# A ring of stationary operands set 192 bytes into its tiles, and eight sums of squares with 64 moving columns

## The chip, the core and the metric

The kernel runs on one core of a Trainium2 chip, in one launch. The metric is the device time of the whole program in microseconds; the median of three runs before the change is 837.2 us (836.03 to 839.48). TensorE (PE in the profile) multiplies: a weight load (PEld) puts a stationary operand of 128x128 into the array, and a matmul then streams the moving operand's columns past it into PSUM. VectorE is DVE, ScalarE is ACT, GpSimd is POOL, and SP issues most DMAs.

## The reference

Linear attention without a softmax, RMS normalisation per head, and a feed-forward block with GELU, all in fp32:

```python
kv  = np.einsum('bhsd,bhse->bhde', k, v)          # 8 batches, 8 heads, 576 tokens, 64 wide
out = np.einsum('bhsd,bhde->bhse', q, kv)
rms = np.sqrt(np.mean(out * out, axis=-1, keepdims=True) + 1e-06)
x   = (out / rms * g_norm)                        # taken as 4608 tokens x 512
h   = x @ w_in                                    # 512 -> 2048
g   = 0.5 * h * (1.0 + erf(h / sqrt(2)))
return g @ w_out                                  # 2048 -> 512
```

## The kernel before

The 4608 tokens go through in nine chunks of 512 (`CH`), eight heads as four pairs. Products of fp32 accuracy are made of three fp32r matmuls with split operands: high with high, low with high, high with low. A fp32r matmul is one pass of the array; one of plain fp32 stands in the profile as two.

The prologue treats the first chunk. Ten plain products of the zero tile `warm` (`keep_warm`, L638) keep TensorE going until the first loads land. A product of one row of ones with one row of `eps` (L691) lays D times epsilon over the first 48 columns of a PSUM tile `sums`. The kv sums (`sum_kv`, L151), the projections (`project_first`, L672) and their squares on ScalarE follow. For pairs 2 and 3 `sum_squares` (L683) adds the squares up with TensorE: a block of 128 tokens is the stationary operand, and `heads`, two columns of ones and noughts, is the moving operand; it writes two columns of `sums` for each of eight blocks. `rsqrt` works on the 48 columns, and products with `ident` (L739) spread the result.

The first two chunks (`PLAIN`) run with weight tiles that are split on the way: `layer1` (L529) and `layer2` (L555), both with 512 moving columns. Meanwhile sums of weight blocks are written to DRAM tiles called `products`.

The other seven chunks (from chunk 2 on) take the first layer by `layer1_pair`: for each of eight pairs j of blocks it does seven products of half size, each of six fp32r matmuls of 256 moving columns (L436). That is 42 matmuls a pair, 56 pairs, 2352 matmuls. The stationary operand of such a product comes from a ring of four tiles, `w_in0` to `w_in3`, filled in turn from `products` by `load_products` (L419); the moving operand is a split piece of x, which lies in the tiles x0 to x5 or w_in5 to w_in12. Behind a pair come the projections of the next chunk (`project`, L211) in some places, then 24 matmuls of layer 2 with 512 columns. The order is written out by hand; every engine works in the order of its own code, SP's loads too.

All tiles lie behind one another in SBUF in the order in which their names first occur, each at a start address of its own, the same in every partition. A tile of the ring has 4096 bytes a partition, as has every weight tile. The starts in the built program, in bytes of a partition, and the rest when divided by 256:

| tiles | role | start before | rest |
|---|---|---|---|
| w_in0, w_in1, w_in2, w_in3 (ring) | stationary in L436 | 59072, 63168, 71360, 91840 | 192 |
| x0 to x5 | moving in L436 and L529 | 157376 to 177856, steps of 4096 | 192 |
| w_in5 to w_in9; w_in10 to w_in12 | moving in L436 in even; in odd chunks | 108224 to 140992, steps of 8192; 26304, 79552, 153280 | 192 |
| kv_h0, kv_h1, kv_l0, kv_l1 | stationary in L211 | 16512, 18560, 20608, 22656 | 128 |
| qh, ql, w_in4 | moving in L211 | 198592, 200640, 100032 | 192 |
| gh, gl | stationary in L555 | 202688 and on | 192 |
| w_out0 to w_out15 | moving in L555 | 67264 and others | 192 |

Within these tiles the operands of L436 and L555 begin at multiples of 512 bytes, those of L211 at multiples of 256 bytes. So in L436, L529 and L555 a stationary and a moving operand have the same rest; in L211 the rests are 128 and 192.

Of the kernel before, what the change touches and what calls it, by code (L numbers as in the profile page):

```python
# [8 lines left out]
F32 = mybir.dt.float32  # L9
F32R = mybir.dt.float32r  # L10
I32 = mybir.dt.int32
AF = mybir.ActivationFunctionType
# [4 lines left out]
P = 128  # L17
EPS = 1e-6
CH = 512
KROWS = 112  # L20
WARM = 10
PLAIN = 2
HALF = CH // 2
RING = 4
# [11 lines left out]
def linear_attn_rms_gelu_ffn(  # L36
# [16 lines left out]
    nc = tc.nc  # L53
    ctx.enter_context(tc.manual_schedule())
    NT, DM = out.shape
# [5 lines left out]
    NF = w_in.shape[0]  # L61
# [4 lines left out]
    const = ctx.enter_context(tc.tile_pool(name="const", bufs=1))  # L66
# [6 lines left out]
    HI, LO = slice(0, DM), slice(DM, 2 * DM)  # L73
    kv_h = [const.tile([P, NP, P], F32R, name=f"kv_h{s}") for s in range(2)]
    kv_l = [const.tile([P, NP, P], F32R, name=f"kv_l{s}") for s in range(2)]
    ident = const.tile([P, P], F32, name="ident")
    fold = const.tile([P, P], F32, name="fold")
    warm = const.tile([P, P], F32, name="warm")
    half_g = const.tile([P, 1], F32, name="half_g")
    heads = const.tile([P, 2], F32, name="heads")  # L80


    kv_in, late = {}, {}
# [1 line left out]
    def late_tile(name):  # L85

        if name not in late:
            late[name] = const.tile([P, 2 * DM], I32, name=name).bitcast(F32)
        return late[name]
# [18 lines left out]
    def load_kv(b, p):  # L108

        early = b == 0 or (b == 1 and p > 1)  # L110
        if early:
            main = late_tile(f"w_out{NF - 1 - p if b == 0 else NF - 3 - p}")
        elif b == PLAIN + 1 and p > 1:
            main = const.tile([P, 2 * DM], F32, name=f"w_in{8 + p}")
# [9 lines left out]
        else:  # L124
            if early:
                tail = late_tile(f"w_in{NF - 5}")[:, (p - 2) * 2 * P:(p - 1) * 2 * P]
            elif b == PLAIN + 1 and p > 1:
                if p == 2:
# [38 lines left out]
    class Attn:  # L167
# [22 lines left out]
        def split_q(self, p, eng=nc.gpsimd):  # L190
            q = self.q.pop(p)
            if self.c > PLAIN and p % 2:
                t = const.tile([P, 2 * DM], F32R, name="w_in4")
# [150 lines left out]
    kept = {}  # L344

    def reused(i, dtype=F32):

        if i not in kept:
            kept[i] = const.tile([P, 2 * DM], dtype, name=f"w_in{i}")
        return kept[i]  # L350

    def piece_tile(c, n):
        k = (["x2", "x3"] + [f"w_in{i}" for i in range(5, 10)],
# [40 lines left out]
    def high_sums():  # L394

        for (j, second), s in stage.items():
            if j % 2:
                t = reused(second, F32R).rearrange("p (k a n) -> p k a n", k=2, a=2)
            else:
                t = const.tile([P, 2, 2, HALF], F32R, name=f"x{2 + second}")  # L400
            nc.scalar.copy(out=t[:, :, 0], in_=s)
            halved[j, second] = s, t
        stage.clear()
# [10 lines left out]
    ring = {}  # L414

    def load_products(t):
        if t < (NCH - PLAIN) * NT2:
            ring[t] = reused(t % RING, F32R)
            nc.sync.dma_start(out=ring[t].bitcast(F32), in_=products[t % NT2])  # L419

    def layer1_pair(at, j, between):
# [8 lines left out]
        def product(k, out, first=False):  # L430
            n = ((at.c - PLAIN) * NF // 2 + j) * NPR + k
            w, x = ring[n // 2][:, n % 2 * DM:(n % 2 + 1) * DM], at.x[k]
            for kb in range(2):
                hi, lo = (w[:, m * HALF + kb * P:m * HALF + (kb + 1) * P] for m in range(2))
                for i, (y, z) in enumerate(((hi, 0), (lo, 0), (hi, 1))):
                    nc.tensor.matmul(  # L436
                        out=out, lhsT=y, rhs=x[:, z, kb], start=first and kb + i == 0,
                        stop=kb == 1 and i == 2, skip_group_check=True,
                    )
            if n % 2:  # L440
                load_products(n // 2 + RING)
# [25 lines left out]
    raw, parts = {}, {}  # L467

    def load_w(n):
        kind, i = weights[n]  # L470
        src = w_in[i] if kind == "in" else w_out[i * P:(i + 1) * P, :]
        raw[n] = const.tile([P, 2 * DM], I32, name=f"w_{kind}{i}")
        nc.sync.dma_start(out=raw[n], in_=src.bitcast(I32))

    zs, ws = {}, {}
# [27 lines left out]

    def high_w(n):
        kind, i = weights[n]
        t = const.tile([P, 2 * DM], F32R, name=f"w_{kind}{i}")
        parts[kind, i] = t
        nc.scalar.copy(out=t[:, HI], in_=ws[n].bitcast(F32))

# [89 lines left out]

    attn = [Attn(c) for c in range(NCH)]  # L600
    first, second = attn[:2]
    nc.vector.memset(warm, 0.0)
    nc.scalar.activation(out=heads, in_=warm[:, :2], func=AF.Gelu)
    mask, g_row = late_tile(f"w_in{NF - 6}")[:, :P], late_tile(f"w_in{NF - 6}")[:1, P:2 * P]
    nc.gpsimd.memset(mask, 0.0)
    ones, eps = (late_tile(f"w_in{NF - 6}")[:1, a * P:(a + 1) * P] for a in (2, 3))
# [10 lines left out]
    for h in range(2):  # L617
        nc.scalar.dma_start(out=g_row[:, h * D:(h + 1) * D], in_=g_norm.unsqueeze(0))
    load_w(0)
    for p in range(2):  # L620
        load_kv(1, p)
    for n in (1, 2, 3):
        load_w(n)
    for p in (2, 3):
        load_kv(1, p)
    load_w(4)
    second.load(0)
    for n in range(5, 9):
# [7 lines left out]
    def keep_warm(count):  # L636
        for _ in range(count):
            nc.tensor.matmul(out=dummy[:, :P], lhsT=warm, rhs=warm, start=True, stop=True)  # L638

    sums = ps_h.tile([P, CH], F32, name="ps_h")  # L640
    dummy = ps_h.tile([P, CH], F32, name="ps_h")
    keep_warm(WARM)
    nc.gpsimd.memset(heads, 0.0)
# [5 lines left out]
    for d in range(0, 2 * D, BLK):  # L649
        h = d // D * D  # L650
        nc.gpsimd.tensor_tensor(
            out=fold[:, d:d + BLK], in0=ident[:, h:h + BLK], in1=ident[:, h + BLK:h + 2 * BLK],
# [7 lines left out]
    sq, NG = {}, CH // P  # L660
# [17 lines left out]
    n = 2 * NB  # L678


    def sum_squares(p):
        for k in range((p - 2) * NG, (p - 1) * NG):
            nc.tensor.matmul(  # L683
                out=sums[:, n + 2 * k:n + 2 * k + 2],
                lhsT=sq[p][:, k % NG * P:(k % NG + 1) * P], rhs=heads, start=False, stop=True,
                skip_group_check=True,
            )

    first.part = work.tile([P, NP, NB], F32, name="part")

    nc.tensor.matmul(  # L691
        out=sums[:, :n + 4 * NG], lhsT=ones, rhs=eps[:, :n + 4 * NG], start=True, stop=False,
        skip_group_check=True,
    )
    sum_first(0)
# [3 lines left out]
        out=half_g, in0=ps[:, :1], scalar1=0.5, scalar2=None, op0=ALU.mult  # L699
# [3 lines left out]
        out=root_g, in0=half_g, scalar1=D ** 0.5, scalar2=None, op0=ALU.mult  # L703
# [8 lines left out]
    for p in (2, 3):  # L712
        project_first(p)
    top_w(0)
    bits_w(0)
    sum_squares(2)
    nc.tensor.matmul(
        out=sums[:, :n].rearrange("p (g b) -> p g b", g=2), lhsT=fold, rhs=first.part[:, :2, :],
        start=False, stop=True, skip_group_check=True,
    )  # L720
    sum_squares(3)
    for p in (2, 3):
        nc.scalar.activation(
            out=first.o_tile(p), in_=first.ps.pop(p), func=AF.Copy, scale=root_g
# [9 lines left out]
    for p in (2, 3):  # L734
        bcs[p] = ps_acc.tile([P, DM], F32, name=f"acc{p}")
        for t in range(NG):
            for h, r in enumerate((slice(0, D), slice(D, 2 * D))):
                k = n + 2 * ((p - 2) * NG + t) + h
                nc.tensor.matmul(  # L739
                    out=bcs[p][r, t * P:(t + 1) * P],  # L740
                    lhsT=first.inv[:, k:k + 1].broadcast_to((P, D)), rhs=ident,
                    start=True, stop=True,
                )
    for p in range(2):
# [3 lines left out]
            out=first.o_tile(p), in0=first.ps.pop(p), scalar=root_g, in1=bc, op0=ALU.mult,  # L748
# [16 lines left out]
    g, h, acc, sums = {}, {}, {}, {}  # L765
# [90 lines left out]
    def convert(i, gelu_rest, between):  # L856

        count = 3 if i in (2, 4, 6, 8) else 2 if i < 11 else i in (11, 12, 14)  # L860
        now = [order.pop(0) for _ in range(count)]
        for k, n in enumerate(now or [None]):
            if last:
                high_w(last[0])
                if last[0] + 2 < len(weights):
                    top_w(last[0] + 2)
            if not i and not k:
                gelu_rest()
                low_w(last.pop())
            if n is not None:  # L870
                bits_w(n)
            if i and not k:
                gelu_rest()
            if last:
                low_w(last.pop())
            if n is not None:
                last.append(n)
            if not k:
                between()
# [6 lines left out]

    for s in range(PLAIN * NF):
        c, i = divmod(s, NF)
# [7 lines left out]
        if c == 0:  # L896
# [4 lines left out]
            def between():  # L901
                if i == 0:
                    for p in (2, 3):
                        attn[0].low_x(p, nc.vector)
                if i in (9, 10):
                    high_w(i - 9)
                    low_w(i - 9)
                if i == 1:
                    split_kv(1, range(NP))
                    nc.scalar.copy(out=kv_h[0], in_=kv_f)  # L910
                    nc.vector.tensor_tensor(
                        out=kv_l[0], in0=kv_f, in1=kv_h[0].bitcast(F32), op=ALU.subtract
                    )
                spread_work(c, i)
# [9 lines left out]
        else:  # L924
# [3 lines left out]
            n = 0 if not 1 <= i <= 11 else 2 if i in (1, 3, 5, 7, 11) else 1  # L928
# [114 lines left out]
```

## Time and profile before

The profiled execution took 835.6 us, of which the span that the profile covers is 833.8 us; 1.8 us lie around it.

| what | value |
|---|---|
| runs | 836.03, 837.2, 839.48 us |
| profiled execution | 835.6 us, span 833.8 us, mean granted clock 0.999 |
| TensorE matmuls | 5386, 828.9 us busy |
| DVE, ACT, POOL busy | 495.9, 314.2, 65.5 us |
| DMA | 174.97 MB, mean 210 GB/s |

A matmul's own duration in the profile includes its way through the array, so the durations of consecutive matmuls overlap. What a matmul costs in a stream is the time from its start to the start of the next. The timeline gives starts in us; a row that merges x24 matmuls gives the start of the first.

### The profile page before, as it was taken

Reading aid. Unit: us, or ns where it says so; the run is one execution under the profiler, and the core shown is the slowest. Engines: PE = TensorE matmul, PEld = TensorE weight load, DVE = VectorE, ACT = ScalarE, POOL = GpSimd, SP = SyncE. Lnnn points to the kernel's source line nnn. Section 1 sums busy time; section 2 is a strip of 40 time slices with the busy share of each in tenths; the row PEclk is TensorE's granted clock in tenths of the full one; section 3 lists DMA queues with packets and bytes.
Section 4 is the critical chain, followed back from the end, with each engine's and each line's share of the span. In section 5 each row is a group of like instructions: output and inputs, shape, how many; then the busy total and the mean of one; then the engine's idle time right before and its main releaser. Section 6 shows DMA issues by size and latency. Waiting matters only on the chain.

```text
span 833.8 us, 13801 instructions
## 1 busy us (share of the span) xinstructions
PE 828.9 (99%) x5386; PEld 735.0 (88%) x5386; DVE 495.9 (59%) x980; ACT 314.2 (38%) x578; POOL 65.5 (8%) x69
## 2 busy tenths in 40 slices
PE   9999999999999999999999999999999999999998
PEld 7688888888999999999999999999999989999997
DVE  3999838687546744674457545673467446744443
ACT  3788444434532334233423253233323332322221
POOL 1000021011000101010001010010101000100000
PEclk9999999999999999999999999999999999999999
DMA  9981347776784568455945587456555655556551
GB/s 348 407 330 51 114 135 250 254 245 240 252 304 135 180 230 307 161 177 202 339 159 176 199 281 262 151 177 229 172 172 172 232 188 177 177 177 227 177 177 51
DMA packets 61605, 174.97 MB, mean 210 GB/s; under 512 B 6500, under 2 KB 15460, under 8 KB 61540
## 3 DMA queue, kind: packets, MB, share of 16 engines
q1 hardware_dynamic: 61536, 174.09, 60.0%
q8 instruction: 43, 0.70, 0.3%
q14 instruction: 22, 0.18, 0.1%
q10 hardware_dynamic: 4, 0.00, 0.0%
HBM read 149.95 MB, written 24.12 MB: 209 GB/s over the span
## 4 chain that ended last, share of the span: by engine, by line
PE 99%; DVE 0%; issue 0%; ACT 0%; DVEq 0%
PE acc L555 47%; PE ps_h L436 34%; PE ps_h L529 10%; PE ps_a L211 3%; PE ps_a L151 2%; PE ps_h L521 1%; PE ps_h L638 1%; PE acc L672 0%; PE acc L739 0%; PE ps_h L683 0%; PE ps_a L241 0%; DVE w L594 0%; DVE w_in L664 0%; PE ps_h L691 0%; DVE sq L583 0%
## 5 line engine op out<-in xcount | busy, mean ns | idle before, releaser
L555 PE MATMUL acc<-w_out,gh 128*128 128x512 f32 x700 | 217.0, 391 | 0.0
L436 PE MATMUL ps_h<-w_in,w_in 128*128 128x256 f32 x1392 | 176.2, 283 | 0.0
L436 PEld LDWEIGHTS ps_h<-w_in,w_in 128*128 128x128 f32 x1392 | 171.1, 192 | 0.0
L555 PE MATMUL acc<-w_out,w_in 128*128 128x512 f32 x672 | 159.7, 392 | 0.0
L555 PEld LDWEIGHTS acc<-w_out,gh 128*128 128x128 f32 x700 | 129.3, 188 | 25.5
L555 PEld LDWEIGHTS acc<-w_out,w_in 128*128 128x128 f32 x672 | 124.0, 188 | 24.8
L555 PE MATMUL acc<-w_out,gl 128*128 128x512 f32 x350 | 136.3, 390 | 0.0
L541 ACT ACTIVATE gh<-ps_h 128x512 fp32r<-128x512 f32 x88 | 52.7, 599 | 212.6 <-DVE ps_h L428 155.4
L436 PEld LDWEIGHTS ps_h<-x,w_in 128*128 128x128 f32 x960 | 122.6, 191 | 4.4
L436 PE MATMUL ps_h<-x,w_in 128*128 128x256 f32 x960 | 123.9, 283 | 0.0
L541 ACT ACTIVATE w_in<-ps_h 128x512 fp32r<-128x512 f32 x56 | 33.6, 600 | 184.7 <-DVE ps_h L428 184.7
L446 DVE COPY w_in<-ps_h 128x256 f32<-128x256 f32 x56 | 23.8, 425 | 133.1 <-PE ps_h L436 133.1
L428 DVE TENSOR_TENSOR ps_h<-ps_h,w_in 128x256 f32<-128x256 f32 x168 | 72.7, 432 | 48.0 <-PE ps_h L436 43.6
L428 DVE TENSOR_TENSOR w_in<-ps_h,w_in 128x256 f32<-128x256 f32 x168 | 71.4, 425 | 49.2 <-PE ps_h L436 47.2
L529 PE MATMUL ps_h<-x,w_in 128*128 128x512 f32 x360 | 86.8, 390 | 0.0
L547 DVE TENSOR_TENSOR gl<-ps_h,gh 128x512 fp32r<-128x512 f32 x88 | 60.4, 687 | 42.4 <-ACT ps_h L542 38.0
L542 ACT ACTIVATE ps_h<-ps_h 128x512 f32<-128x512 f32 x144 | 85.5, 594 | 0.0
L529 PEld LDWEIGHTS ps_h<-x,w_in 128*128 128x128 f32 x360 | 67.4, 188 | 13.9 <-POOL x L299 0.2
L555 PEld LDWEIGHTS acc<-w_out,gl 128*128 128x128 f32 x350 | 65.7, 188 | 14.1
L547 DVE TENSOR_TENSOR w_in<-ps_h,w_in 128x512 fp32r<-128x512 f32 x56 | 38.4, 686 | 17.1 <-ACT ps_h L542 17.1
L199 POOL TENSOR_TENSOR ql<-q,qh 128x512 fp32r<-128x512 f32 x16 | 21.1, 1321 | 211.5 <-ACT qh L198 140.9
L334 POOL TENSOR_TENSOR w_in<-o,w_in 128x512 fp32r<-128x512 f32 x13 | 16.9, 1325 | 210.8 <-ACT w_in L329 210.8
(153 smaller groups left out, 640.4 us busy)
## 6 DMA issues: line engine op xcount, KB each, us to landing
w_in<-products SPq DMA_DIRECT2D x196, 512.0 KB, 4.6
products<-w_in SPq DMA_DIRECT2D x40, 256.0 KB, 3.0
w_in<-w_in SPq DMA_DIRECT2D x16, 512.0 KB, 10.2
kv_main<-kv_main SPq DMA_DIRECT2D x16, 512.0 KB, 7.0
w_out<-w_out SPq DMA_DIRECT2D x16, 512.0 KB, 10.2
q<-qT SPq DMA_DIRECT2D x15, 512.0 KB, 5.7
out<-w SPq DMA_DIRECT2D x18, 256.0 KB, 2.1
out<-z SPq DMA_DIRECT2D x17, 256.0 KB, 2.3
```

Source lines behind the costliest of these rows:

```text
L151: nc.tensor.matmul(out=ps[r, n * D:(n + 1) * D], lhsT=k[:, r], rhs=v[:, r], start=(j == 0), stop=(j == NJ),)
L199: eng.tensor_tensor(out=ql, in0=q, in1=qh.bitcast(F32), op=ALU.subtract)
L211: nc.tensor.matmul(out=ps[:, a:e], lhsT=w, rhs=x[:, a:e], start=(m == 0), stop=(m == 2))
L334: eng.tensor_tensor(out=x[:, 1], in0=self.block(OPERANDS[n]), in1=x[:, 0].bitcast(F32), op=ALU.subtract,)
L428: add = lambda out, x, y: nc.vector.tensor_tensor(out=out, in0=x, in1=y, op=ALU.add)
L436: nc.tensor.matmul(out=out, lhsT=y, rhs=x[:, z, kb], start=first and kb + i == 0, stop=kb == 1 and i == 2, skip_group_check=True,)
L446: nc.vector.tensor_copy(out=p1, in_=a[:, left])
L529: nc.tensor.matmul(out=h, lhsT=parts["in", i][:, w][:, p * P:(p + 1) * P], rhs=at.x[p][:, x], start=(m + p == 0), stop=(m == 2 and p == NP ...
L541: nc.scalar.activation(out=gh, in_=h, func=AF.Gelu)
L542: nc.scalar.activation(out=h, in_=h, func=AF.Gelu)
L547: nc.vector.tensor_tensor(out=gl, in0=h, in1=gh.bitcast(F32), op=ALU.subtract)
L555: nc.tensor.matmul(out=ps, lhsT=x[:, ts], rhs=parts["out", i][:, w], start=(i == 0 and m == 0), stop=(m == 2 and (i == NF - 1 or (i, t) == ...
```

## The change

Three things change in the code.

1. **The ring.** The four ring tiles get 64 more fp32 columns (256 bytes). `load_products` writes a product pair 48 columns (192 bytes) behind the tile's start, and the products read it there. What else uses these tiles still begins at their start.
2. **The sums of squares.** `heads` gets 72 columns, all nought but the first two. `sum_squares` streams the first 64 of them and so writes 64 columns of `sums`, the last 62 with an addend of nought. The product with `eps` covers 128 columns in place of 48, so that all of these columns are begun.
3. **Room.** `ident` and `warm` (512 bytes each) give up tiles of their own and lie in the tile w_in10, which is loaded with weights later.

```diff
+WIDE = 64
-    ident = const.tile([P, P], F32, name="ident")
-    warm = const.tile([P, P], F32, name="warm")
-    heads = const.tile([P, 2], F32, name="heads")
+    heads = const.tile([P, 72], F32, name="heads")
+    AWAY, ROOM = 48, 64
+    def block_tile(name, dtype):
+        ring = name in [f"w_in{i}" for i in range(RING)]
+        return const.tile([P, 2 * DM + (ROOM if ring else 0)], dtype, name=name)
...
     def load_products(t):
         if t < (NCH - PLAIN) * NT2:
-            ring[t] = reused(t % RING, F32R)
+            reused(t % RING, F32R)
+            ring[t] = kept[t % RING][:, AWAY:AWAY + 2 * DM]
             nc.sync.dma_start(out=ring[t].bitcast(F32), in_=products[t % NT2])
...
+    ident = late_tile(f"w_in{NF - 6}")[:, DM + 2 * P:DM + 3 * P]
+    warm = late_tile(f"w_in{NF - 6}")[:, DM + P:DM + 2 * P]
...
         for k in range((p - 2) * NG, (p - 1) * NG):
             nc.tensor.matmul(
-                out=sums[:, n + 2 * k:n + 2 * k + 2],
-                lhsT=sq[p][:, k % NG * P:(k % NG + 1) * P], rhs=heads, start=False, stop=True,
+                out=sums[:, n + 2 * k:n + 2 * k + WIDE],
+                lhsT=sq[p][:, k % NG * P:(k % NG + 1) * P], rhs=heads[:, :WIDE], start=False, stop=True,
                 skip_group_check=True,
             )
...
-        out=sums[:, :n + 4 * NG], lhsT=ones, rhs=eps[:, :n + 4 * NG], start=True, stop=False,
+        out=sums[:, :P], lhsT=ones, rhs=eps, start=True, stop=False,
```

In the built program the ring's tiles now start at 58304, 62656, 71104 and 91840, again with a rest of 192, so a product's stationary operand, 192 bytes further, has a rest of 128. Every other tile in the table keeps its rest. The pair of rests in L436 is now 128 and 192, as in L211.

No engine gets its instructions in another order. TensorE's rows around the sums of squares (`ql` and `gh` hold the squares of pairs 2 and 3, `part` the reduced squares of pairs 0 and 1) stood before as

```order
L672 MATMUL acc_315<-w_in_130,w_in_153 128x512
L683 MATMUL ps_h<-heads,ql 128x2 x4
L717 MATMUL ps_h<-part,fold 128x32
L683 MATMUL ps_h<-heads,gh 128x2 x4
L638 MATMUL ps_h<-warm 128x128 x2
```

and stand now as

```order
L682 MATMUL acc_313<-w_in_128,w_in_151 128x512
L694 MATMUL ps_h<-heads,ql 128x64 x4
L728 MATMUL ps_h<-part,fold 128x32
L694 MATMUL ps_h<-heads,gh 128x64 x4
L648 MATMUL ps_h<-w_in_109 128x128 x2
```

Only the shape of eight rows and the name of the zero tile differ. The first pair of chunk 2 reads the ring (the right one of the two operands) before as

```order
L436 MATMUL ps_h<-x_1971,w_in_1483 128x256 x6
L436 MATMUL ps_h<-x_2068,w_in_1483 128x256 x6
L436 MATMUL ps_h<-w_in_2071,w_in_1492 128x256 x6
L436 MATMUL ps_h<-w_in_2152,w_in_1492 128x256 x6
L436 MATMUL ps_h<-w_in_2017,w_in_2049 128x256 x6
L436 MATMUL ps_h<-w_in_2020,w_in_2049 128x256 x6
L436 MATMUL ps_h<-w_in_2155,w_in_2051 128x256 x6
```

and now, with the same count, shapes and order,

```order
L444 MATMUL ps_h<-x_1969,w_in_1481 128x256 x6
L444 MATMUL ps_h<-x_2066,w_in_1481 128x256 x6
L444 MATMUL ps_h<-w_in_2069,w_in_1490 128x256 x6
L444 MATMUL ps_h<-w_in_2150,w_in_1490 128x256 x6
L444 MATMUL ps_h<-w_in_2015,w_in_2047 128x256 x6
L444 MATMUL ps_h<-w_in_2018,w_in_2047 128x256 x6
L444 MATMUL ps_h<-w_in_2153,w_in_2049 128x256 x6
```

The load of w_in10 with weights waits for TensorE's last read of `ident` besides the engines that it waited for; the product that reads `g_norm`'s row (L697) waits for ScalarE besides its DMAs.

More of the change, by code (lines that the diff above doesn't have):

```diff
@@ L348, in reused @@
         if i not in kept:
-            kept[i] = const.tile([P, 2 * DM], dtype, name=f"w_in{i}")
-        return kept[i]
+            kept[i] = block_tile(f"w_in{i}", dtype)
+        return kept[i][:, :2 * DM]
     def piece_tile(c, n):
@@ L471, in load_w @@
         src = w_in[i] if kind == "in" else w_out[i * P:(i + 1) * P, :]
-        raw[n] = const.tile([P, 2 * DM], I32, name=f"w_{kind}{i}")
+        raw[n] = block_tile(f"w_{kind}{i}", I32)[:, :2 * DM]
         nc.sync.dma_start(out=raw[n], in_=src.bitcast(I32))
@@ L505, in high_w @@
         kind, i = weights[n]
-        t = const.tile([P, 2 * DM], F32R, name=f"w_{kind}{i}")
+        t = block_tile(f"w_{kind}{i}", F32R)[:, :2 * DM]
         parts[kind, i] = t
@@ L601, in linear_attn_rms_gelu_ffn @@
     first, second = attn[:2]
+    ident = late_tile(f"w_in{NF - 6}")[:, DM + 2 * P:DM + 3 * P]
+    warm = late_tile(f"w_in{NF - 6}")[:, DM + P:DM + 2 * P]
     nc.vector.memset(warm, 0.0)
-    nc.scalar.activation(out=heads, in_=warm[:, :2], func=AF.Gelu)
+    nc.scalar.activation(out=heads[:, :2], in_=warm[:, :2], func=AF.Gelu)
     mask, g_row = late_tile(f"w_in{NF - 6}")[:, :P], late_tile(f"w_in{NF - 6}")[:1, P:2 * P]
```

## The prediction

> **What bounds the kernel.** First the page: span, engines, and the chain that ended last by line.
>
> ```profile
> span 833.8 us, 13801 instructions
> PE 828.9 (99%) x5386; PEld 735.0 (88%) x5386; DVE 495.9 (59%) x980; ACT 314.2 (38%) x578; POOL 65.5 (8%) x69
> PE 99%; DVE 0%; issue 0%; ACT 0%; DVEq 0%
> PE acc L555 47%; PE ps_h L436 34%; PE ps_h L529 10%; PE ps_a L211 3%; PE ps_a L151 2%; PE ps_h L521 1%; PE ps_h L638 1%; PE acc L672 0%; PE acc L739 0%; PE ps_h L683 0%; PE ps_a L241 0%; DVE w L594 0%; DVE w_in L664 0%; PE ps_h L691 0%; DVE sq L583 0%
> ```
>
> TensorE holds 99% of the chain, and 34% of it is L436, the line whose stationary operands are moved. The costliest groups and the waits of TensorE come next.
>
> ```profile
> L436 PE MATMUL ps_h<-w_in,w_in 128*128 128x256 f32 x1392 | 176.2, 283 | 0.0
> L436 PE MATMUL ps_h<-x,w_in 128*128 128x256 f32 x960 | 123.9, 283 | 0.0
> PE ps_h L638 <- DVE warm L602: 1.1, 1, 1.1
> PE acc L672 <- DVE w_in L664: 0.6, 2, 0.4
> ```
>
> 1392 + 960 = 2352 matmuls with no idle time before them; all that TensorE waits in its own row is 1.7 us, in the prologue. So no other engine has to become faster for TensorE to go on, and what a matmul of L436 costs is its step, from its start to the next start. That is read from the timeline, TensorE alone, of the second pair of a chunk and what follows it (start, length, then the group).
>
> ```profile
> 307.29 3.04 PE L436 MATMUL ps_h<-x,w_in 128*128 128x256 f32 x24
> 310.17 2.32 PE L436 MATMUL ps_h<-w_in,w_in 128*128 128x256 f32 x18
> 312.33 0.28 PE L211 MATMUL ps_a<-w_in,kv_h 128*128 128x256 f32 x1
> ```
>
> 24 matmuls from 307.29 to 310.17 are 120.0 ns each, the next 18 to 312.33 also 120.0. A run of 42 takes 5.04 us, and 56 runs 282.2 us.
>
> **The change, part by part: the ring.** L436 keeps its count, shapes and order. What differs is where the weight load reads: before, stationary and moving operand had the same rest by 256 (192 and 192), now 128 and 192. Nothing in L436 of before shows that. L211 does: projections with the same 256 columns in fp32r, the same three-product pattern, rests 128 and 192. Two places with 256 columns, the first right behind L436, the second behind L555:
>
> ```profile
> 301.15 0.28 PE L211 MATMUL ps_a<-qh,kv_h 128*128 128x256 f32 x1
> ...
> 301.71 0.28 PE L211 MATMUL ps_a<-ql,kv_h 128*128 128x256 f32 x1
> 301.83 0.63 PE L555 MATMUL acc<-w_out,gh 128*128 128x512 f32 x2
> ...
> 313.01 2.91 PE L555 MATMUL acc<-w_out,w_in 128*128 128x512 f32 x12
> 315.75 0.28 PE L211 MATMUL ps_a<-qh,kv_h 128*128 128x256 f32 x1
> ...
> 316.34 0.28 PE L211 MATMUL ps_a<-ql,kv_h 128*128 128x256 f32 x1
> 316.46 2.89 PE L555 MATMUL acc<-w_out,w_in 128*128 128x512 f32 x12
> ```
>
> The first place: six matmuls (the middle four left out here) from 301.15 to 301.83, 113.3 ns each. The second: five steps from 315.75 to 316.34, 118.0 ns each. Same operands, same rests, same length; what differs is what ran before. A third place, from 312.33 to 313.01, again behind L436, has six matmuls at 113.3 ns. The two values bound the gain (an end below nothing stands with the rivals): 120.0 - 118.0 = 2.0 ns a matmul or 120.0 - 113.3 = 6.7 ns. I take 118.0, since each run of L436 is entered from layer 2's matmuls, as the second place is (the row at 313.01 ends where it starts), and its steps show no drift towards 113.3. A run would take 42 x 0.118 = 4.956 us in place of 5.04, 0.084 us less, and 56 runs **4.7 us less**. With 113.3 a run takes 4.759, 0.281 less, and 56 runs 15.7 us less.
>
> The loads into the ring stand so in the page:
>
> ```profile
> w_in<-products SPq DMA_DIRECT2D x196, 512.0 KB, 4.6
> ```
>
> They keep their size and their waits, so nothing behind them in SP's queue is moved. With a run shorter by 0.1 to 0.3 us they have that much less time; they land in a median of 4.6 us from their issue, and a ring of four holds two to three more loads than the one in use. DVE takes the results of L436 and is 59% busy, so it follows.
>
> At this place a rule of the Trainium skill speaks against the change. "TensorE: Matmul & The Clock Gate", in the section "Step-by-step: what each phase is for", says of TensorE's two read ports: "Loading the next tile's weights doesn't steal SBUF read bandwidth from the running matmul." By that rule the place of the stationary operand would not matter, and the time would stay. The same page, section "Back-to-back issue gap", gives a step of columns / 2.4 + 2.5 ns, an estimate of 109 ns for 256 columns; the trace's 120.0 lies above it, and so does its 113.3 where the rests differ, so the rule does not agree well with the rows, but no run yet has moved one operand alone.
>
> **The sums of squares.** 16 passes (two for each plain fp32 product) stream 64 columns in place of 2.
>
> ```profile
> 5.63 0.66 PE L691 MATMUL ps_h<-w_in 1*128 1x48 f32 x2
> 6.22 0.78 PE L151 MATMUL ps_a<-w_out 112*64 112x64 f32 x16
> ...
> 14.19 1.04 PE L683 MATMUL ps_h<-heads,ql 128*128 128x2 f32 x8
> 15.09 0.39 PE L717 MATMUL ps_h<-part,fold 128*128 128x32 f32 x2
> 15.32 1.03 PE L683 MATMUL ps_h<-heads,gh 128*128 128x2 f32 x8
> 16.21 0.36 PE L638 MATMUL ps_h<-warm 128*128 128x128 f32 x1
> 20.57 7.22 PE L521 MATMUL ps_h<-o,w_out 128*128 128x512 f32 x16
> 27.73 0.69 PE L151 MATMUL ps_a<-w_out 112*64 112x64 f32 x16
> ```
>
> Eight passes take 14.19 to 15.09, 112 ns each with 2 columns, and the two of L717 with 32 columns 115: a new weight load of 128 columns comes with each, and it covers the columns. 64 columns of plain fp32 stream in about 56 ns (L521: 16 passes of 512 columns in 7.16 us, 447 ns each, an eighth of that). So they stay under the 112 ns of cover, and I cost them at nothing. Were the cover gone, 16 x 56 = 0.9 us would be the other end.
>
> **The product with `eps`** has 80 more columns in two passes, while the array is still slow:
>
> ```profile
> 1.06 4.64 PE L638 MATMUL ps_h<-warm 128*128 128x128 f32 x20 [1.06 <-DVE warm L602]
> ```
>
> L638's first 20 passes of 128 columns take 1.06 to 5.63, 229 ns each. 80 columns are 143 ns a pass, **0.3 us** in all, and I count them in full, since TensorE carries the chain through the prologue; the other end is nothing, if a load of kv is what L151 waits for then.
>
> **Room and waits.** POOL's memset of `heads` grows from 2 to 72 columns; L691 waits for the memsets behind it, which end long before TensorE gets there.
>
> ```profile
> 2.36 0.11 POOL L643 MEMSET heads<- 128x2 f32 x1 [1.03 <-ACT heads L603]
> 2.94 0.19 POOL L647 MEMSET w_in<- 1x128 f32 x1
> 2.04 0.20 ACT L603 ACTIVATE heads<-warm 128x2 f32<-128x2 f32 x1
> 7.05 0.38 PE L697 MATMUL ps_a<-heads,w_in 1*128 1x1 f32 x2
> 18.68 1.97 PE L739 MATMUL acc<-ident,y 128*64 128x128 f32 x32
> 38.91 0.33 SPq L473 DMA_DIRECT2D w_in<-w_in  x1
> ```
>
> The last of these memsets ends at 3.13, L691 starts at 5.63. SP's load of w_in10 is, by its place in SP's order, the one issued at 38.91; its new wait, for L739's read of `ident`, is over at 20.65. ScalarE's write of `heads` ends at 2.24, and L697, which now waits for ScalarE, runs at 7.05. All of this costs nothing; if one of the covers failed, it would be some tenths of a microsecond.
>
> **Sum.** 835.6 (span 833.8 and 1.8 around it) - 4.7 + 0.3 = 831.2 us on the scale of the profiled execution. The median of the runs, 837.2, lies 1.6 above that execution and the lowest 0.4; I add 0.8, half of the former, and forecast **832.0 us**.
>
> **The rivals.**
> *The faster step holds.* If the phase of 301.15 sets in in each run, 113.3 ns, the sum is 835.6 - 15.7 + 0.3 + 0.8 = 821.0. For it: two of the three places with 256 columns in L211 look like this one. Against it: both come right behind L436, where a run of L436 itself never starts.
>
> *Nothing comes of it.* The short steps of L211 may have another cause than the rests (it writes other PSUM tiles and reads other moving tiles), or the phase slides back to 120.0 over 42 matmuls, of which L211 shows only six. The sum is 835.6 + 0.3 + 0.8 = 836.7. The rule of "TensorE: Matmul & The Clock Gate" in the Trainium skill, quoted above, would give this case.
>
> *Slower.* The new rests may make the collision worse. With 512 columns they do:
>
> ```profile
> 292.71 3.56 PE L555 MATMUL acc<-w_out,w_in 128*128 128x512 f32 x15
> 296.11 3.04 PE L436 MATMUL ps_h<-x,w_in 128*128 128x256 f32 x24
> ...
> 673.59 0.39 PE L211 MATMUL ps_a<-qh,kv_h 128*128 128x512 f32 x1
> ...
> 674.05 0.39 PE L211 MATMUL ps_a<-ql,kv_h 128*128 128x512 f32 x1
> 674.28 0.39 PE L555 MATMUL acc<-w_out,w_in 128*128 128x512 f32 x1
> ```
>
> 15 steps of L555, equal rests, are 226.7 ns; three of L211, rests 128 and 192, are 230. If a long run of L436 settled 3.3 ns above its 120.0, it would add 2352 x 3.3 = 7.8 us: 844.5. It decides from 120.1 ns on. Against it: no 256-column place shows more than 118.0.
>
> **How the numbers follow.** Chances: 118 ns (832.0) 0.42; 113.3 ns (821.0) 0.30; no gain (836.7) 0.17; slower (844.5) 0.11. About 0.5%, 4.2 us, is what a measurement of this kernel can tell from no change, so faster means under 833.0 and slower over 841.4. All of the second case and two thirds of the first are faster: 0.58; slower 0.11; the rest, 0.31, within. The range goes from the second case less 1 us, 820.0, to 836.8, which takes in half of the third; it leaves out the slower case and the other half.
>
> **What would show it.** In the changed profile the steps of L444 (L436 before) between its 24-row and its 18-row: 118, 113.3, 120.0 or over. If all 56 runs show one value, address alone sets it; if some show 113 and others 118, entry does. L694's eight passes should still take 0.90 us, L702 about 0.3 us more. Wrong would be: steps of L563 that move too, although their rests did not change, or TensorE waiting for the ring's loads at the head of a product.

## The result, and the profile after

The changed kernel takes 830.51 us, median of 8 runs (829.68 to 834.36); the kernel before, beside it, 837.05 (8 runs, 835.7 to 841.06). The ratio is 0.9926, with an interval of 0.9901 to 0.9950: 6.2 us less by the ratio, between 4.2 and 8.3. The profiled execution was the longest of the eight, 834.36 us, with a prologue 4.27 us longer than that of the trace of before; so the two traces are compared from the first matmul of layer 2 on.

The page of the changed kernel: span, engines, chain by engine and by line.

```profile
span 832.6 us, 13801 instructions
PE 827.9 (99%) x5386; PEld 732.7 (88%) x5386; DVE 496.3 (60%) x980; ACT 314.2 (38%) x578; POOL 65.7 (8%) x69
PE 99%; DVE 0%; ACT 0%; issue 0%; DVEq 0%
PE acc L563 47%; PE ps_h L444 33%; PE ps_h L537 10%; PE ps_a L218 3%; PE ps_a L158 3%; PE ps_h L529 1%; PE acc L682 1%; PE ps_h L648 1%; PE acc L750 0%; PE ps_h L694 0%; PE ps_a L248 0%; PE ps_h L702 0%; DVE w L602 0%; PE ps_a L708 0%; DVE sq L591 0%; DVE z L592 0%
```

Nothing has moved to another engine: the same lines in the same order (L555 is now L563, L436 is L444, L211 is L218), and L444 went from 34 to 33%. The costliest groups, and the waits of TensorE:

```profile
L444 PE MATMUL ps_h<-w_in,w_in 128*128 128x256 f32 x1392 | 173.0, 279 | 0.0
L444 PE MATMUL ps_h<-x,w_in 128*128 128x256 f32 x960 | 122.2, 279 | 0.0
PE ps_h L648 <- DVE w_in L612: 1.1, 1, 1.1
PE acc L682 <- DVE w_in L674: 0.4, 1, 0.4
```

L444 has still no idle time before it, so TensorE doesn't wait for the ring; its matmuls are 279 ns long in place of 283. What they cost is read from their starts in the timeline, for the second pair of a chunk as before, and for the projections behind another pair:

```profile
304.55 0.28 PE L218 MATMUL ps_a<-qh,kv_h 128*128 128x256 f32 x1
...
305.26 0.63 PE L563 MATMUL acc<-w_out,gh 128*128 128x512 f32 x2
...
310.70 2.99 PE L444 MATMUL ps_h<-x,w_in 128*128 128x256 f32 x24
313.53 2.28 PE L444 MATMUL ps_h<-w_in,w_in 128*128 128x256 f32 x18
315.65 0.28 PE L218 MATMUL ps_a<-w_in,kv_h 128*128 128x256 f32 x1
```

24 matmuls from 310.70 to 313.53 are 117.9 ns each, the next 18 to 315.65 are 117.8: the step of 118 that the forecast took, in place of 120.0. Added up by starts, all 56 runs of L444 last 4.944 to 4.947 us (before 5.032 to 5.035), and the 2352 matmuls 276.93 us (before 281.85). The six projections from 304.55 to 305.26, whose operands and rests did not change, take 118 ns each where the first place of the prediction showed 113.3: they now run behind L444's new state.

The prologue, which hides the gain in this execution, before:

```profile
7.59 1.12 PE L672 MATMUL acc<-w_in,w_in 128*128 128x512 f32 x2 [0.16 <-DVE w_in L664]
8.64 0.69 PE L151 MATMUL ps_a<-w_out 112*64 112x64 f32 x16
...
29.05 0.72 PE L555 MATMUL acc<-w_out,gh 128*128 128x512 f32 x2
```

and in the changed kernel:

```profile
5.63 0.79 PE L702 MATMUL ps_h<-w_in 1*128 1x128 f32 x2
6.35 1.12 PE L158 MATMUL ps_a<-w_out 112*64 112x64 f32 x16
...
8.16 2.08 PE L682 MATMUL acc<-w_in,w_in 128*128 128x512 f32 x2
10.16 1.12 PE L158 MATMUL ps_a<-w_out 112*64 112x64 f32 x16
...
16.23 2.39 PE L682 MATMUL acc<-w_in,w_in 128*128 128x512 f32 x4
18.46 1.10 PE L694 MATMUL ps_h<-heads,ql 128*128 128x64 f32 x8
19.40 0.36 PE L728 MATMUL ps_h<-part,fold 128*128 128x32 f32 x2
...
33.32 0.73 PE L563 MATMUL acc<-w_out,gh 128*128 128x512 f32 x2
```

Two passes of 512 columns last 1.00 us each (8.16 to 10.16), against 0.52 before (7.59 to 8.64). Layer 2 begins at 33.32, 4.27 us later. The list of the granted clock in the trace file fits this: full clock begins in it at 17.09 us here and at 6.46 before. By their starts, the first of the four passes at 16.23 takes 0.94 us, and the three from 17.17 on take 0.43 each. In the traces of the seven kernels below, whose tiles are moved as here, full clock begins between 4.04 and 6.55 us. This speaks against the change as the cause of the late clock; what the cause is isn't shown. The kernel with the ring alone begins layer 2 at 29.00. From the start of layer 2 to the end of the span are 832.6 - 33.32 = 799.28 us, before 833.8 - 29.05 = 804.75: 5.47 less. By starts L444 has 4.92 of it, and L563 0.68 (393.89 to 393.21 us in all); L218's 256-column steps give back 0.07 (2.74 to 2.82).

### The profile page after: what moved, and what is told of

Read it like the earlier page. It is cut to its first block, busy times and chain, and to the rows that moved or that the text cites. A ratio compares the mean times of both kernels' runs of the same rounds, so it can differ in the third digit from the quotient of the medians.

```text
span 832.6 us, 13801 instructions
## 1 busy us (share of the span) xinstructions
PE 827.9 (99%) x5386; PEld 732.7 (88%) x5386; DVE 496.3 (60%) x980; ACT 314.2 (38%) x578; POOL 65.7 (8%) x69
## 4 chain that ended last, share of the span: by engine, by line
PE 99%; DVE 0%; ACT 0%; issue 0%; DVEq 0%
PE acc L563 47%; PE ps_h L444 33%; PE ps_h L537 10%; PE ps_a L218 3%; PE ps_a L158 3%; PE ps_h L529 1%; PE acc L682 1%; PE ps_h L648 1%; PE acc L750 0%; PE ps_h L694 0%; PE ps_a L248 0%; PE ps_h L702 0%; DVE w L602 0%; PE ps_a L708 0%; DVE sq L591 0%; DVE z L592 0%
## 5 line engine op out<-in xcount | busy, mean ns | idle before, releaser
L563 PE MATMUL acc<-w_out,gh 128*128 128x512 f32 x700 | 216.7, 391 | 0.0
L444 PE MATMUL ps_h<-w_in,w_in 128*128 128x256 f32 x1392 | 173.0, 279 | 0.0
L444 PEld LDWEIGHTS ps_h<-w_in,w_in 128*128 128x128 f32 x1392 | 167.8, 188 | 0.0
L563 PE MATMUL acc<-w_out,w_in 128*128 128x512 f32 x672 | 159.3, 391 | 0.0
L563 PEld LDWEIGHTS acc<-w_out,gh 128*128 128x128 f32 x700 | 129.2, 188 | 25.3
L563 PEld LDWEIGHTS acc<-w_out,w_in 128*128 128x128 f32 x672 | 123.9, 188 | 24.6
L563 PE MATMUL acc<-w_out,gl 128*128 128x512 f32 x350 | 136.3, 389 | 0.0
L444 PEld LDWEIGHTS ps_h<-x,w_in 128*128 128x128 f32 x960 | 120.9, 188 | 4.3
L444 PE MATMUL ps_h<-x,w_in 128*128 128x256 f32 x960 | 122.2, 279 | 0.0
L436 DVE TENSOR_TENSOR ps_h<-ps_h,w_in 128x256 f32<-128x256 f32 x168 | 72.7, 433 | 46.1 <-PE ps_h L444 42.2
L436 DVE TENSOR_TENSOR w_in<-ps_h,w_in 128x256 f32<-128x256 f32 x168 | 71.4, 425 | 46.8 <-PE ps_h L444 44.9
L555 DVE TENSOR_TENSOR gl<-ps_h,gh 128x512 fp32r<-128x512 f32 x88 | 60.4, 687 | 41.9 <-ACT ps_h L550 37.5
L563 PEld LDWEIGHTS acc<-w_out,gl 128*128 128x128 f32 x350 | 65.7, 188 | 13.9
L555 DVE TENSOR_TENSOR w_in<-ps_h,w_in 128x512 fp32r<-128x512 f32 x56 | 38.4, 686 | 17.1 <-ACT ps_h L550 17.1
```

The costliest lines, as they stand in the source:

```text
L436: add = lambda out, x, y: nc.vector.tensor_tensor(out=out, in0=x, in1=y, op=ALU.add)
L444: nc.tensor.matmul(out=out, lhsT=y, rhs=x[:, z, kb], start=first and kb + i == 0, stop=kb == 1 and i == 2, skip_group_check=True,)
L555: nc.vector.tensor_tensor(out=gl, in0=h, in1=gh.bitcast(F32), op=ALU.subtract)
L563: nc.tensor.matmul(out=ps, lhsT=x[:, ts], rhs=parts["out", i][:, w], start=(i == 0 and m == 0), stop=(m == 2 and (i == NF - 1 or (i, t) == ...
```

## The experiments

The theory: the difference between the rests of the stationary and of the moving operand sets the step of L444, and what ran before chooses between 118 and 113.3 ns. The rivals: the stationary operand's own place sets it; or the sums of squares have a part in the time. Below, "N apart" means that the start of the stationary operand less that of the moving one leaves a rest of N bytes when divided by 256: none in L436 before, 192 in L444 and in the projections. A product whose operands are none apart is called equal.

**The ring alone.** The sums of squares go back to 2 columns, the product with `eps` to 48; the ring stays 192 bytes in.

```diff
-                out=sums[:, n + 2 * k:n + 2 * k + WIDE],
-                lhsT=sq[p][:, k % NG * P:(k % NG + 1) * P], rhs=heads[:, :WIDE], start=False, stop=True,
+                out=sums[:, n + 2 * k:n + 2 * k + 2],
+                lhsT=sq[p][:, k % NG * P:(k % NG + 1) * P], rhs=heads[:, :2], start=False, stop=True,
...
-        out=sums[:, :P], lhsT=ones, rhs=eps, start=True, stop=False,
+        out=sums[:, :n + 4 * NG], lhsT=ones, rhs=eps[:, :n + 4 * NG], start=True, stop=False,
```

> The ring's offset and the moved tiles stay, the sums of squares go back to 2 moving columns and the product with eps to 48. If the ring is the whole gain (step of the first layer's products 117.7 ns in place of 120.0, 2352 of them, 4.9 us): ratio to before about 0.994, step 117.7. If the wide sums are what gains (by the clock in the prologue): step 117.7 in the profile but ratio above 0.997.

Measured: 830.27 us (6 runs, 829.89 to 831.6), ratio 0.9924 (0.9905 to 0.9943). Its timeline:

```profile
5.63 0.66 PE L702 MATMUL ps_h<-w_in 1*128 1x48 f32 x2
6.21 0.82 PE L158 MATMUL ps_a<-w_out 112*64 112x64 f32 x16
...
29.00 0.72 PE L563 MATMUL acc<-w_out,gh 128*128 128x512 f32 x2
...
306.53 2.99 PE L444 MATMUL ps_h<-x,w_in 128*128 128x256 f32 x24
309.36 2.28 PE L444 MATMUL ps_h<-w_in,w_in 128*128 128x256 f32 x18
311.48 0.28 PE L218 MATMUL ps_a<-w_in,kv_h 128*128 128x256 f32 x1
```

The steps are those of the changed kernel (2.83 us for 24, 2.12 for 18), and from layer 2 to the end of the span (828.4) it is 799.4 us, as there. The ring makes the gain. The product with `eps` takes 0.58 us with 48 columns (5.63 to 6.21) and 0.72 with 128.

**The wide sums alone.** The ring's tiles keep their size, and the products begin at the tile's start.

```diff
-    AWAY, ROOM = 48, 64
+    AWAY, ROOM = 0, 64
```

> Ring at the tiles' start again (rests by 256 equal), wide sums and moved tiles stay. If the ring is the whole gain: step 120.0 ns, ratio 0.999 to 1.001. If the wide sums gain by themselves some 1 to 2 us in the prologue: step 120.0, ratio about 0.998.

Measured: 836.27 us (12 runs, 835.71 to 839.97), ratio 1.0001 (0.9984 to 1.0017). Its timeline:

```profile
29.67 0.73 PE L563 MATMUL acc<-w_out,gh 128*128 128x512 f32 x2
...
307.88 3.04 PE L444 MATMUL ps_h<-x,w_in 128*128 128x256 f32 x24
310.75 2.32 PE L444 MATMUL ps_h<-w_in,w_in 128*128 128x256 f32 x18
312.92 0.28 PE L218 MATMUL ps_a<-w_in,kv_h 128*128 128x256 f32 x1
```

18 matmuls from 310.75 to 312.92 are 120.6 ns each by the rounded starts, 120.0 by the unrounded ones; from layer 2 to the end it is 834.4 - 29.67 = 804.7 us, as before. The wide sums and the moved tiles make no difference that 12 runs show.

**Both operands moved.** A pad of 64 bytes ahead of all tiles but those of kv, `fold` and `half_g`: in L445 (L444's place) the stationary rest is 192 now and the moving rest 0, so they stay 192 apart, while the projections (L219) become 128 apart.

```diff
+    const.tile([P, 16], F32, name="pad")
```

> As the changed kernel, with 64 bytes of padding ahead of all tiles but kv_h and kv_l: stationary operands of the ring get rest 192, moving ones rest 0, so the difference stays 192 and both places change; the projections' difference becomes 128. If the difference of the two sets the step: 117.7 ns again. If the place of the stationary operand by itself does (rest 128 good, 192 bad): 120.0 ns. The projections with 256 columns: 118 if any unequal rest does, another value if the amount counts.

Measured: 830.36 us, one run. Its timeline:

```profile
300.15 0.27 PE L219 MATMUL ps_a<-qh,kv_h 128*128 128x256 f32 x1
...
300.87 0.62 PE L564 MATMUL acc<-w_out,gh 128*128 128x512 f32 x2
...
306.31 2.99 PE L445 MATMUL ps_h<-x,w_in 128*128 128x256 f32 x24
309.14 2.28 PE L445 MATMUL ps_h<-w_in,w_in 128*128 128x256 f32 x18
311.26 0.27 PE L219 MATMUL ps_a<-w_in,kv_h 128*128 128x256 f32 x1
```

L445's steps are again 117.9 and 117.8 ns with the stationary rest at 192, where before it gave 120.0: not its own place counts but its distance from the moving operand. The projections, now 128 apart, take 0.72 us for six (300.15 to 300.87), 120 ns each in place of 118.

**The first product of a pair at equal rests.** In the kernel before, each run of L436 began with a step of 113.3 ns, then 119.1, then settled at 120.0; the changed one is at 118 from its first step. The idea: let the first of a pair's seven products run with equal rests, and move to 192 apart while it is in that state. Where a load of two products would bridge different places, it becomes two loads.

```diff
-            ring[t] = kept[t % RING][:, AWAY:AWAY + 2 * DM]
-            nc.sync.dma_start(out=ring[t].bitcast(F32), in_=products[t % NT2])
+            at = [0, AWAY + DM] if 2 * t % NPR == 0 else [AWAY, AWAY + DM]
+            if (2 * t + 1) % NPR == 0:
+                at[1] = ROOM + DM
+            ring[t] = [kept[t % RING][:, a:a + DM] for a in at]
...
-            w, x = ring[n // 2][:, n % 2 * DM:(n % 2 + 1) * DM], at.x[k]
+            w, x = ring[n // 2][n % 2], at.x[k]
```

> As the changed kernel, but the first of the seven products of each pair lies so that its rests are equal, the other six 192 apart (28 of 98 loads of the ring's cycle go as two DMAs). If what ran before sets which of two steps holds, as the projections behind L436 suggest: 113, 119 and four of 120.0 for the first product, then 113.3 for the other 36, 4.79 us a run in place of 4.945, 8.7 us less in all, ratio to before about 0.982. If address difference alone sets the step: 120 then 117.7, about 0.8 us more than the changed kernel, ratio 0.994.

Measured: 823.23 us (6 runs, 822.64 to 826.35), ratio 0.9841 (0.9818 to 0.9865): faster than both kernels. Its timeline:

```profile
306.51 2.92 PE L453 MATMUL ps_h<-x,w_in 128*128 128x256 f32 x24
309.27 2.20 PE L453 MATMUL ps_h<-w_in,w_in 128*128 128x256 f32 x18
311.31 0.28 PE L218 MATMUL ps_a<-w_in,kv_h 128*128 128x256 f32 x1
```

18 matmuls from 309.27 to 311.31 are 113.3 ns each, at the places at which the changed kernel needs 117.8. The 24 of the first row average 115.0: by starts the first six are 113.3, 119.1, 120.0, 120.0, 120.0, 120.9, all others 113.3. Each of the 56 runs lasts 4.793 to 4.795 us, together 268.43, 8.5 less than in the changed kernel. So one distance has two steps, and what came before chooses. This also says what the projections' short step hung on: right behind L436, whose products are equal, they took 113.3 ns, and right behind L444, whose products are 192 apart, 118. Here, behind this kernel's short state, they take 113.3 again (311.31 and on). So it is how the products ahead ran that counts, and not their line.

**Eight pairs, eight patterns.** The kernel of the last experiment with a table of distances: each pair of a chunk has its own, the same in all seven chunks.

```diff
+    def rest_of(j, k):
+        whole = {5: 0, 6: 16, 7: 32}
+        one = {(0, 0): 0, (2, 0): 16, (3, 1): 0, (4, 0): 32}
+        return whole[j] if j in whole else one.get((j, k), AWAY)
```

`j` is the pair, `k` the product, and the numbers are columns of 4 bytes.

> The difference of rests differs from pair to pair of each chunk. Pair 0: first product 0, the others 192. Pair 1: all 192. Pair 2: first product 64, the others 192. Pair 3: second product 0, the others 192. Pair 4: first product 128, the others 192. Pair 5: all 0. Pair 6: all 64. Pair 7: all 128. If a product with equal rests switches what follows: pair 0 goes 120 then 113.3, pair 1 117.7 throughout, pair 3 117.7, then 120, then 113.3, pair 5 120. If the first product of a pair has to be the equal one: pair 3 goes back to 117.7. Of 64 and 128 nothing is known but the projections at 128 (112 to 124 ns, mean 119): pair 7 about 119, pair 6 between 113 and 120 if the amount counts at all.

Measured: 831.66 us, one run. The timeline of three pairs of one chunk:

```profile
295.35 2.92 PE L458 MATMUL ps_h<-x,w_in 128*128 128x256 f32 x24
298.11 2.20 PE L458 MATMUL ps_h<-w_in,w_in 128*128 128x256 f32 x18
300.15 0.28 PE L218 MATMUL ps_a<-qh,kv_h 128*128 128x256 f32 x1
...
363.49 2.99 PE L458 MATMUL ps_h<-x,w_in 128*128 128x256 f32 x24
366.31 2.28 PE L458 MATMUL ps_h<-w_in,w_in 128*128 128x256 f32 x18
...
373.91 3.05 PE L458 MATMUL ps_h<-x,w_in 128*128 128x256 f32 x24
376.79 2.32 PE L458 MATMUL ps_h<-w_in,w_in 128*128 128x256 f32 x18
```

The first 24 steps of pair 0 (first product equal) average 115.0 ns, of pair 6 (all 64 apart) 117.5, of pair 7 (all 128 apart) 120.0. All eight, from the starts of each matmul (the sum of 42 steps, and the mean step of products):

| pair | distance | 42 steps, us | first product | others |
|---|---|---|---|---|
| 0 | first none, others 192 | 4.793 | 118.9 | 113.3 |
| 1 | all 192 | 4.947 | 117.8 | 117.8 |
| 2 | first 64, others 192 | 4.949 | 118.2 | 117.8 |
| 3 | second none, others 192 | 4.947 | 117.4 | second 118.3, then 117.8 |
| 4 | first 128, others 192 | 4.971 | 121.2 | 117.8 |
| 5 | none | 5.032 | 118.7 | 120.0 |
| 6 | all 64 | 4.947 | 117.8 | 117.8 |
| 7 | all 128 | 5.049 | 121.1 | 120.0 (in turn 117.3, 120.0, 122.7) |

64 and 192 apart give the same. An equal product brings the short step when it stands first (pair 0), not when it stands second (pair 3), and neither 64 nor 128 apart in the first product does (pairs 2 and 4).

**Layer 2 moved.** Does the same help where 512 columns stream? A pad ahead of the work tiles moves gh and gl, the stationary operands of 1050 matmuls of layer 2, against their moving operands: 64 apart in one kernel, 192 in the other. It moves the other work tiles as well, qh and ql of the projections among them. The ring is as in the changed kernel.

```diff
+    work.tile([P, 16], F32, name="pad")
```

> As the changed kernel, with 64 bytes of padding ahead of the tiles of gh and gl, so that 1050 of layer 2's 1722 matmuls (512 columns) have rests 64 apart, the other 672 equal ones. If unequal rests help there as in the first layer (2.3 ns a step): 1050 steps of about 224.4 in place of 226.7, 2.4 us less. If with 512 columns they cost, as the projections did at 192 (230): about 3.5 us more. If 512 columns don't care: 226.7.

```diff
+    work.tile([P, 48], F32, name="pad")
```

> The same with 192 bytes of padding: 1050 matmuls of layer 2 at 192, and the projections from qh and ql with equal rests. From the projections with 512 columns at 192 (229 to 230 ns): 1050 steps of about 229.5, 3 us more. If long runs behave otherwise than three matmuls: 226.7 or less. The projections with 256 columns and equal rests: 120 where they were 117.7.

Measured: 839.07 us with 64 apart and 832.99 with 192, one run each. From layer 2 to the end of the span it is 806.9 and 801.1 us, against 799.3 in the changed kernel: 7.6 and 1.9 more. The timeline with 64 apart, a stretch with moved operands:

```profile
354.80 0.63 PE L564 MATMUL acc<-w_out,gh 128*128 128x512 f32 x2
...
358.29 2.99 PE L445 MATMUL ps_h<-x,w_in 128*128 128x256 f32 x24
```

and the stretch that answers to it in the changed kernel:

```profile
353.88 0.62 PE L563 MATMUL acc<-w_out,gh 128*128 128x512 f32 x2
...
357.28 2.99 PE L444 MATMUL ps_h<-x,w_in 128*128 128x256 f32 x24
```

15 matmuls from 354.80 to 358.29 are 232.7 ns each, and 226.7 where the rests are equal (353.88 to 357.28). Over all 1050 such steps the means are 233.9 ns at 64 apart and 229.8 at 192, against 228.0 for the same steps in the changed kernel, whose rests are equal: with 512 columns both distances that were tried lose. The projections with equal rests, in the kernel with 192, did not show the expected 120 ns: the six at 302.26 average 118.5 and the six at 316.91 118.3. Six are few, since the first six of pair 5, all equal, average 118.7 as well.

The kernel with 192 apart showed one more thing. Its timeline at two runs of L445 in one chunk:

```profile
386.46 1.58 PE L445 MATMUL ps_h<-x,w_in 128*128 128x256 f32 x12
387.88 3.70 PE L445 MATMUL ps_h<-w_in,w_in 128*128 128x256 f32 x30
391.41 0.31 PE L219 MATMUL ps_a<-qh,kv_h 128*128 128x320 f32 x1
...
397.69 1.52 PE L445 MATMUL ps_h<-x,w_in 128*128 128x256 f32 x12
399.05 3.56 PE L445 MATMUL ps_h<-w_in,w_in 128*128 128x256 f32 x30
402.44 0.30 PE L219 MATMUL ps_a<-w_in,kv_h 128*128 128x320 f32 x1
```

The first run takes 118 ns a step (30 from 387.88 to 391.41), the second 113.0 (30 from 399.05 to 402.44), with the same distances and no equal product in either. Two of this kernel's 56 runs took the short step, this one and the one at 487.0. In both, the weight load of the first matmul started 229 ns ahead of it; in the 54 runs that went to 118 it was 222 to 227. That lead doesn't settle the step, though. In the kernel with layer 2 at 64 apart 28 of 56 runs were entered with a lead of 229 or 230 ns, and all went to 118; in the kernel whose first product is equal the lead was 223 or 224, and the short step followed in all 56. So the entry decides, but what it is in the entry stays open. An equal product as the first of a run is the one way found that brings the short step every time.

## Why the prediction was right

**The ring, 4.7 us.** Right in place and in size: 4.92 measured. The difference is the step's mean, 117.74 in place of 118 ns, and the old one, 119.83 in place of 120.0.

**The choice of 118 over 113.3.** Right, and the reason given, that a run of L444 is entered from layer 2, fits all 56 runs. It is not the whole of it: entered from layer 2 with its operands 192 apart, two of 56 runs took 113. The sign that was named for telling the two causes apart, one value in all 56 runs for the address alone, could not do so: all 56 runs are entered alike. That 113.3 was there to be had at the same addresses is shown by the kernel whose first product is equal. It gains 13.6 us by its median, between 11.3 and 15.2 by its interval, near to the 15.7 that the rival counted, since each run pays for the first product: 4.793 us in place of 4.759.

**No term for what lies around L444.** Missed, and small: L563 lost 0.68 us, and the projections behind L444 went from 113.3 to 118, 0.07 us more. Moving steps of L563 had been named as a sign of being wrong. Their starts show where they moved: the first five steps of the 32 stretches that come right behind L444 lost 0.56 us together (the second went from 235.7 to 230.8 ns), while the median of all its steps stayed at 227.

**The product with eps, 0.3 us.** Mis-sized: 0.13 measured, 0.72 us against 5.63 to 6.22, 0.59, before. The first pass grew by 0.127 us, near the 0.143 of the term; the second, from its start to L158, grew by 0.006 alone, and what hid its columns isn't shown. Both executions were still at the slow clock there. In the five kernels of the experiments whose full clock began before this product (at 4.04 to 5.15 us), the same 128 columns took 0.41 us, so the term's size hangs on when the clock comes.

**Sums of squares at nothing.** Right within what runs can tell: eight passes took 0.94 us (18.46 to 19.40) in place of 0.90, and the kernel with the wide sums alone has a ratio of 1.0001, whose interval is at most 1.4 us to either side.

**The median's offset, 0.8 us.** A guess, and it was not there: the kernel with the ring alone was profiled at 830.28 us, and its median is 830.27. The 832.0 came out 1.5 us too high; the offset is half of this, L563 most of the other half.

**The rule that spoke against it.** The Trainium skill says in "TensorE: Matmul & The Clock Gate", section "Step-by-step: what each phase is for", that loading the next weights doesn't take read bandwidth from the running matmul. The rival that follows from it, no gain, did not come: with the same instructions a step is 120.0, 117.7 or 113.3 ns (256 columns), by where the two operands lie to each other and by the entry. That it is read bandwidth which is lost is not shown.

**Open.** Why the distance counts, and where in the memory the two reads would meet, was not found; distances were tried in steps of 64 bytes alone. Nor was it found what in the entry chooses between 118 and 113.3, or why the full clock came late in the changed kernel's profiled execution.

## What to carry to other kernels

Where TensorE's chain is all matmuls with a new weight load each, measure the step from start to start, and compare places with the same shape but other operand addresses: their difference may be a gain to be had by moving a tile. Try the distance for each number of columns on its own, since 192 bytes won 2% of the step with 256 columns and lost 1% with 512. Look at the first steps of a run too: the short step of 113.3 ns that each run lost after its first matmul was worth more here, once it was made to last, than the one that the addresses gave.

## What the runs showed of the hardware

- The same matmuls at the same addresses have two lasting steps, 113.3 and 117.7 ns; the short one lasts for at least 36 matmuls and goes over to the projections behind them (113.3 behind the short state, 118 behind the long one). Behind equal products, which take 120.0 themselves, the projections take 113.3 too.
- 64 and 192 bytes apart are alike with 256 columns (117.8 ns), 128 apart is as slow as equal rests (120.0) and goes in threes, 117.3, 120.0, 122.7. With 512 columns equal rests are the shortest of the three that were tried: means of 228.0 ns, 229.8 at 192 and 233.9 at 64.
- In the changed kernel's profiled execution the page's row of the granted clock shows 9, which is 90% of full speed or more, in every slice, while passes of 512 columns took 0.94 to 1.02 us until 17.17 us and 0.43 from there on. The list of the clock in the trace file begins at 17.09: the row does not show this slow start.
